# Window attention and a sticky mixture of experts on one core: a list's last products placed later in the order, the first branch target announced earlier, and the weight subtractions shared out evenly

## The chip, the core and the metric

The kernel runs on one core of a Trainium2 chip. The core has five engines with instruction streams of their own: TensorE (PE in the profile, its weight loads PEld), VectorE (DVE), ScalarE (ACT), GpSimd (POOL) and SyncE (SP). Streams wait for each other by semaphores. The metric is the device time of one execution in microseconds (us), the median of several.

## What is computed

An attention over 8 batches of 512 local and 32 global tokens gives 4608 rows `x` of 512 numbers. A sticky router then picks one of 8 experts for each row, and two products with that expert's weights make the output:

```python
fresh_e = int(np.argmax(logits[b, s]))
if s == 0 or local_gate[b, s] < 0.5:
    e = fresh_e
else:
    e = prev_e if prev_e >= 0 else fresh_e
prev_e = e
...
h = np.maximum(x[b, s] @ w1[e], 0.0)
out[b, s] = p[e] * (h @ w2[e])
```

`w1[e]` is 512 x 1024 and `w2[e]` 1024 x 512. Which rows go to which expert is known only when the attention and the router are done.

## The kernel before

**Two parts.** Class `Attn` works through the attention and `Route` sorts the rows by expert. `Moe` computes the experts in blocks of up to 256 rows (512 for what is left over): three early blocks (`NX = 3`) of rows that are known before the last batch is routed, then eight "rem" blocks, one for each expert's remainder, then as many full blocks as the data need. In this input there are three full ones.

**One block.** A weight matrix comes in eight pieces of 128 x 1024 floats (four of `w1`, four of `w2`). For each piece `load` issues a DMA on SyncE into a buffer `raw`; `split` lets ScalarE convert it to the rounded half `hi` (a CAST, L1143), and the next `flush` lets VectorE subtract (L1152) to get the rest `lo`. `flush` also issues the load of the next piece. The rows of a block are gathered by GpSimd (L1177), transposed on TensorE in groups of 128 (`xpose`, L1191) and split in the same way: ScalarE copies to `xh` (L1193), VectorE subtracts to `xl` (L1194). `mm1` then makes eight chunks of 12 matmuls (L1226), one for each 128 hidden columns; ScalarE applies the relu to `hh` (L1228), and VectorE makes the rest `hl` (L1229). The three PSUM banks that `mm1` rotates over come free by these two. `mm2` makes eight chunks of three matmuls (L1237) for each group of 128 rows. `store` scales the sum on ScalarE (L1242) and GpSimd scatters it (L1243).

**Order of the last early block.** The last batch's routing and the lists run as a generator, `tail`. After each chunk `hook` takes one step of it, flushes, and makes the splits that the table `SP` names. Inside `tail`, the generator `lists` is stepped twice per hook (`every(..., 2)`). It ends in `pick`: three VectorE operations make one-hots in a buffer in `xT` (L989, L991, L993), then after `wait` empty steps 34 small matmuls on TensorE sum them (L999), and two VectorE operations make the row numbers (L1001, L1002). A second, larger `pick` for the other lists ends at the very end of the third block. `kinds` makes `cnd`, the case of each rem block.

**Rem blocks.** Each rem block is a ten-way switch: `half` for up to 128 rows (case 0), otherwise `part` with `mm1` over 256 to 512 columns. What a case does is called its arm. After the arm, all cases join in the common part `close`: the last eight chunks of `mm2`, two transpositions for the next block, the gather for the block after it, and two splits. Before `close`, `hint` loads `cnd` of the next block into a register on all five engines and announces the branch target (TENSOR_LOAD L1403, BRANCH_PREFETCH_HINT L1409). The branch itself is a COMPARE_BRANCH, shown under L1532 together with other code that the framework adds. An arm makes six splits, `close` two. At the start of the first rem block the ring of `raw` buffers grows from four to eight.

## Time and profile before

| | |
|---|---|
| median of 3 runs | 723.16 us (722.44 to 723.32) |
| the profiled execution | 724.97 us, of which the span from the first to the last instruction is 723.2 us |
| granted TensorE clock, mean | 0.979 |
| TensorE busy | 675.5 us (93%) |
| VectorE, ScalarE, GpSimd busy | 436.8, 345.6, 192.8 us |

The attention fills the first 225 us. The early blocks follow to 333 us and the rem blocks from 336 us. A row of the timeline gives an instruction's start, its duration, its engine, line and operation, the tiles it writes and reads, and how many instructions are merged in the row; in brackets stand the idle time of its engine before it and what ended that. Names are by tile: weights and activations of the rem blocks share `wp`, `wq`, `xh`, `hh` and others by reuse of the memory.

### The profile page before, as it was taken

What the parts mean: (1) busy time and instruction counts of PE and PEld (TensorE: products, weight loads), DVE (VectorE), ACT (ScalarE), POOL (GpSimd) and SP (SyncE); (2) the same over time, 40 slices, a digit from 0 to 9 for tenths busy, and PEclk for the clock granted to TensorE, in tenths of its full rate; (3) what the DMA queues carried; (4) which work ended last, traced back from release to release, by engine and by line L of the source; (5) the groups of instructions that cost most, each with busy time, mean ns of one, the idle gap of its engine ahead of it and who ended that gap; (6) DMA issues with size and microseconds to landing.
All of it is one profiled execution on the core that took longest, in us unless ns stands there. A gap on an engine that the chain in (4) does not pass through costs nothing.

```text
span 723.2 us, 18483 instructions
## 1 busy us (share of the span) xinstructions
PE 675.5 (93%) x7253; PEld 563.5 (78%) x7253; DVE 436.8 (60%) x1142; ACT 345.6 (48%) x614; POOL 192.8 (27%) x321
## 2 busy tenths in 40 slices
PE   8999999999899899698997999999999999999990
PEld 6777777777567869586886888889788889899880
DVE  7868778778787777883527444426263525265660
ACT  4555555554445646352436444335344425255550
POOL 7634434334143110223022303040403020212210
PEclk9999999999999999899998999999999999999996
DMA  8866876966584576668238645445554433366762
GB/s 325 367 245 230 322 281 240 340 253 243 189 311 170 196 235 236 234 199 291 88 128 262 218 165 177 153 168 163 181 191 153 167 133 102 122 211 240 236 207 91
DMA packets 43444, 153.02 MB, mean 212 GB/s; under 512 B 8013, under 2 KB 9293, under 8 KB 39120
## 3 DMA queue, kind: packets, MB, share of 16 engines
q1 hardware_dynamic: 35968, 128.49, 50.2%
q0 software_dynamic: 6960, 21.90, 9.2%
q8 instruction: 77, 1.26, 0.7%
q14 instruction: 151, 1.24, 0.5%
q10 hardware_dynamic: 288, 0.13, 0.1%
HBM read 132.12 MB, written 19.69 MB: 210 GB/s over the span
## 4 chain that ended last, share of the span: by engine, by line
PE 32%; issue 22%; DVE 5%; POOL 3%; ACT 1%; SPq 1%; DMA 0%; POOLq 0%; ACTq 0%; DVEq 0%
PE ps L1237 16%; PE ps L1226 13%; POOL out_dram L1243 2%; PE ps L1191 1%; POOL xr L1177 1%; DVE wp L1152 1%; DVE wq L1152 1%; DMA raw<-in_w_dram 0%; SPq L417 0%; DVE wp L1194 0%; PE ps L999 0%; DVE hl L1229 0%; DVE hl L1152 0%; ACT wp L1143 0%; DVE o L905 0%
## 5 line engine op out<-in xcount | busy, mean ns | idle before, releaser
L1243 POOL DMA_INDIRECT out_dram<-y,tk x39 | 42.0, 1078 | 340.0 <-ACT y L1242 326.9
L1237 PE MATMUL ps<-wp,wq 128*128 128x512 f32 x504 | 128.4, 402 | 1.4 <-ACT wp L1143 1.4
L1226 PE MATMUL ps<-wp,wp 128*128 128x256 f32 (+5 forms) x672 | 111.1, 325 | 4.5 <-issue 2.9
L1226 PEld LDWEIGHTS ps<-wp,wp 128*128 128x128 f32 x672 | 104.8, 190 | 10.3 <-issue 3.5
L1237 PEld LDWEIGHTS ps<-wp,wq 128*128 128x128 f32 x504 | 93.5, 190 | 21.9 <-ACT wp L1143 1.8
L1229 DVE SCALAR_TENSOR_TENSOR wq<-ps,wq 128x256 fp32r<-128x256 f32 (+5 forms) x80 | 41.9, 527 | 98.9 <-ACT wq L1228 91.2
L1228 ACT ACTIVATE wq<-ps 128x256 fp32r<-128x256 f32 (+5 forms) x80 | 36.9, 467 | 89.3 <-PE ps L1226 85.8
L191 POOL TENSOR_SCALAR_AFFINE_SELECT qbd<-raw 64x512 f32<-64x512 f32 x62 | 44.6, 720 | 119.6 <-PE ps L243 101.8
L243 PE MATMUL ps<-kx,qbd 128*64 128x128 f32 x1024 | 71.1, 280 | 3.0 <-issue 2.6
L1242 ACT ACTIVATE y<-ps,pp 128x512 f32<-128x512 f32 x39 | 26.8, 688 | 85.7 <-PE ps L1237 83.9
L243 PEld LDWEIGHTS ps<-kx,qbd 128*64 128x64 f32 x1024 | 54.8, 137 | 12.7 <-issue 8.0
L248 DVE TENSOR_REDUCE mx<-ps 128x4 f32<-128x512 f32 x64 | 43.9, 686 | 29.6 <-PE ps L243 29.6
L1152 DVE TENSOR_TENSOR wp<-raw,wp 128x1024 fp32r<-128x1024 f32 x47 | 57.0, 1216 | 0.0
L254 ACT ACTIVATE pe<-pe 128x512 f32<-128x512 f32 x64 | 40.7, 636 | 32.7 <-DVE pe L250 32.7
L1143 ACT CAST wp<-raw 128x1024 fp32r<-128x1024 f32 x49 | 51.1, 1045 | 6.2 <-DMA raw<-in_w_dram 5.4
L1152 DVE TENSOR_TENSOR wp<-xT,wp 128x1024 fp32r<-128x1024 f32 x16 | 19.6, 1225 | 52.9 <-ACT wp L1143 52.9
L1177 POOL DMA_INDIRECT xr<-xs,idx x32 | 35.4, 1106 | 38.3 <-DVE L L391 17.5
L250 DVE TENSOR_TENSOR pe<-ps,mx 128x512 f32<-128x512 f32 x64 | 44.1, 688 | 1.6
L276 PE MATMUL ps<-v,pt 128*32 128x65 f32 x2048 | 42.6, 222 | 1.9 <-DVE xa L284 0.8
L276 PEld LDWEIGHTS ps<-v,pt 128*32 128x32 f32 x2048 | 33.3, 110 | 13.6 <-issue 7.4
L191 POOL TENSOR_SCALAR_AFFINE_SELECT kx<-raw 128x384 f32<-128x384 f32 (+3 forms) x127 | 42.9, 371 | 3.2 <-DMA raw<-in_qk_dram 1.1
L262 ACT COPY pt<-ps 128x512 f32<-128x512 f32 x64 | 34.9, 610 | 16.9 <-PE ps L260 16.9
(287 smaller groups left out, 1191.8 us busy)
## 6 DMA issues: line engine op xcount, KB each, us to landing
raw<-in_w_dram SPq DMA_DIRECT2D x79, 512.0 KB, 3.4
v<-in_vw_dram SPq DMA_DIRECT2D x32, 1040.0 KB, 8.0
raw<-in_qk_dram SPq DMA_DIRECT2D x32, 528.0 KB, 7.6
xa<-in_w_dram SPq DMA_DIRECT2D x24, 512.0 KB
xT<-in_w_dram SPq DMA_DIRECT2D x24, 512.0 KB
xs<-xa SPq DMA_DIRECT2D x8, 1056.0 KB, 4.5
qgb<-in_qg_dram SPq DMA_DIRECT2D x8, 128.0 KB, 4.8
out_dram<-y,tk POOLq DMA_INDIRECT x39, 4.4
```

The costliest lines, as they stand in the source:

```text
L191: self.nc.gpsimd.affine_select(out=out, in_=in_, pattern=pat, compare_op=ALU.is_ge, fill=0.0, base=0, channel_multiplier=0)
L243: nc.tensor.matmul(sp[64 * t2:64 * t2 + 64, t], qbd[:, w], kf[:, f:f + P], start=False, stop=True, skip_group_check=True)
L248: nc.vector.tensor_reduce(out=mx, in_=st["sp"], axis=AX.X, op=ALU.max)
L250: nc.vector.tensor_tensor(out=st["pe"][:, 4 * hb:4 * hb + 4], in0=st["sp"], in1=mx.broadcast_to([P, 4, P]), op=ALU.subtract)
L276: nc.tensor.matmul(o[32 * w4:32 * w4 + 32, g, h], pt[:, 2 * g + w4 // 2, w4 % 2, h, :], v[:, w, h * (D + 1):(h + 1) * (D + 1)], start=True ...
L1143: nc.scalar.copy(out=hi, in_=raw)
L1152: (nc.gpsimd if pool else nc.vector).tensor_tensor(out=lo, in0=raw, in1=hi.bitcast(F32), op=ALU.subtract)
L1177: self.nc.gpsimd.indirect_dma_start(out=self.xr[j], out_offset=None, in_=src, in_offset=bass.IndirectOffsetOnAxis(ap=self.rt.idx[:, c0 + j ...
L1226: nc.tensor.matmul(ph, a[:, dc, fs], b_[:, dc, n0:n1], start=(n == 0), stop=(n == 11))
L1229: nc.vector.scalar_tensor_tensor(out=hl[:, fc, n0:n1], in0=ph, scalar=0.0, in1=hh[:, fc, n0:n1].bitcast(F32), op0=ALU.max, op1=ALU.subtract)
L1237: nc.tensor.matmul(py, a[:, fc, js], b_[:, fs], start=(fc == 0 and k == 0), stop=(fc == 7 and k == 2))
L1243: sc = nc.gpsimd.indirect_dma_start(out=self.out, out_offset=bass.IndirectOffsetOnAxis(ap=self.g[1][:, j:j + 1], axis=0), in_=y, in_offset ...
```

## The change

1. The first `pick` gets `wait = 12` instead of 2. With two steps of the list per hook, its matmuls come five chunks later on TensorE, and everything of the tail behind it moves as well.
2. In the third early block, `kinds` is run to its end and `hint(i + 1)` is issued after the first chunk of the second row group and not inside its sixth. This puts the hint ahead of the four transpositions for the first rem block.
3. The splits of a rem or full block are now four in the arm and four in `close`, in place of six and two. In `close` the splits come after the transpositions. The last split of `close` is subtracted in the next block's arm.
4. In rem and full blocks the loads no longer follow the subtractions (`eager = False`). The arm issues eight loads, one per chunk of `mm1` except the fifth, and the last in the first chunk of `mm2`. The four extra loads at the end of the third early block go.
5. All four groups of a rem block are gathered into one tile `xr4`, and the three small VectorE operations for each group of rows (the product with the expert's one-hot, the token number, the sum) are done once for all groups (`scals`), at the end of `close`, and not after each transposition.

```diff
-        yield from self.pick(cid, phi, self.o2, 0, 4, 2 * NX, ((0, NT),), po)
+        yield from self.pick(cid, phi, self.o2, 0, 4, 2 * NX, ((0, NT),), po, 12)
...
+        self.eager = True
...
     def flush(self):
         nc = self.nc
-        for pool, raw, hi, lo in self.pend:
+        while self.pend:
+            pool, raw, hi, lo = self.pend.pop(0)
             (nc.gpsimd if pool else nc.vector).tensor_tensor(out=lo, in0=raw, in1=hi.bitcast(F32), op=ALU.subtract)
-            self.load()
-        self.pend = []
-
-    def step(self, n=0):
+            if self.eager:
+                self.load()
+
+    def step(self, n=0, loads=0):
         self.flush()
         for _ in range(n):
             self.split()
+        for _ in range(loads):
+            self.load()
...
+        if i < NX:
+            self.scal(i, j, xr.rearrange("p (o r) -> p o r", o=1))
+
+    def scal(self, i, j, xr):
...
+    def scals(self, i):
+        if i < NSLOT:
+            self.scal(i, 0, self.xr4[:, 0:4 if self.kind(i) == "rem" else 2])
...
         for fc in range(8):
-            if mid and fc == 4:
+            if mid and fc == 1:
                 while not self.known:
                     self.take(next(self.tail))
-            if mid and fc == 6:
                 self.hint(i + 1)
             self.mm2(i, py, fc, 1, *x[2:])
             self.hook(i, 16 + fc)
             if mid and fc in XPM:
                 self.xpose(i + 1, XPM.index(fc))
+                if fc == XPM[-1]:
+                    self.scals(i + 1)
...
+            self.eager = False
             old = [self.raw() for _ in range(4)]
             self.raw.t, self.raw.k = self.more + old, 0
-            for _ in self.more:
-                self.load()
...
-            self.step((2, 1, 1, 1)[k])
+            self.step(1, 2 if k < 3 else 1)
         for j in range(2):
             self.xpose(i + 1, j)
         turn(3)
-        self.step(1)
-        self.step()
+        self.step(0, 1)
...
             self.mm1(i, fc, *x, n0, n1)
-            self.step(fc % 2 == 0)
+            self.step(fc % 2 == 0, fc != 4)
...
                 if g == 0:
-                    self.step(fc in (1, 4))
+                    if fc == 0:
+                        self.step(0, 1)
                     if fc in (2, 5):
                         self.xpose(i + 1, fc // 3)
...
             self.mm2(i, py, fc, j, self.HH, self.HL)
-            self.step(fc in (1, 4))
             if fc in (2, 5):
                 self.xpose(i + 1, 2 + fc // 3)
                 if fc == 5:
+                    self.scals(i + 1)
                     self.gather(i + 2)
+            self.step(fc in (1, 3, 5, 7))
         self.store(py, j)
```

TensorE, the end of the second early block. `ps_64` is the sum of its second row group, two rows a chunk; `L999` are the first list's matmuls, of which the first pair stands here. Before:

```order
L1237 MATMUL ps_64<-wp_100,hh 128x512 x2
L1237 MATMUL ps_64<-wp_100,hl 128x512
L1237 MATMUL ps_64<-wp_101,hh 128x512 x2
L1237 MATMUL ps_64<-wp_101,hl 128x512
L999 LDWEIGHTS o_290
L999 MATMUL ps_69<-xT,o_290 128x8
```

TensorE at the same place now:

```order
L1253 MATMUL ps_64<-wp_101,hh 128x512 x2
L1253 MATMUL ps_64<-wp_101,hl 128x512
L1253 MATMUL ps_64<-wp_4207,hh 128x512 x2
L1253 MATMUL ps_64<-wp_4207,hl 128x512
L1253 MATMUL ps_64<-wp_4207,hh 128x512 x2
L1253 MATMUL ps_64<-wp_4207,hl 128x512
L1253 MATMUL ps_64<-wp_4208,hh 128x512 x2
L1253 MATMUL ps_64<-wp_4208,hl 128x512
L1253 MATMUL ps_64<-wp_4208,hh 128x512 x2
L1253 MATMUL ps_64<-wp_4208,hl 128x512
L999 LDWEIGHTS o_290
L999 MATMUL ps_69<-xT,o_290 128x8
```

The list's matmuls stood after the third chunk of the group and now stand after its eighth, the last one of the block.

VectorE, from the last `hl` of the third early block to the first `xl` of the first rem block (`wp_4311` from `ps_68`). Before:

```order
L1229 SCALAR_TENSOR_TENSOR hl<-ps_65,hh 128x256
L1152 TENSOR_TENSOR wp_4207<-raw_79,wp_4207 128x1024
L1229 SCALAR_TENSOR_TENSOR hl<-ps_66,hh 128x256
L1152 TENSOR_TENSOR wp_4208<-raw_80,wp_4208 128x1024
L1152 TENSOR_TENSOR wp_4312<-raw_77,wp_4312 128x1024
L1152 TENSOR_TENSOR wp_4313<-raw_78,wp_4313 128x1024
L1152 TENSOR_TENSOR xl<-raw_79,xh 128x1024
L1194 TENSOR_TENSOR wp_4311<-ps_68,wp_4209 128x4x128
```

VectorE now, from a little behind the last `hl` (the second large one-hot group and one of the weight subtractions stand ahead of this piece):

```order
L993 TENSOR_SCALAR xT<-xT,ipf 128x8x54
L989 TENSOR_TENSOR xT<-cid,phi 128x8x54
L991 TENSOR_TENSOR xT<-xT,t_264 128x8x54
L993 TENSOR_SCALAR xT<-xT,ipf 128x8x54
L1155 TENSOR_TENSOR wp_4312<-raw_77,wp_4312 128x1024
L1155 TENSOR_TENSOR wp_4313<-raw_78,wp_4313 128x1024
L1155 TENSOR_TENSOR xl<-raw_79,xh 128x1024
L1420 TENSOR_LOAD cnd
L1426 SWITCH_STRIDE
L1426 ISA
L1426 BRANCH_PREFETCH_HINT
L1199 TENSOR_TENSOR wp_4311<-ps_68,wp_4209 128x4x128
```

Of the second list's one-hots, which all stood ahead of the last two `hl`, these and some more are now behind them, and the hint has come between the subtractions and the first `xl`.

ScalarE, `close` of the first rem block; `y` are the two stores of the block, L1193 (now L1198) the copies of the transposed rows. Before:

```order
L1242 ACTIVATE y_4318<-ps_70,pp_92 128x512
L1143 CAST wp_4312<-xT 128x1024
L1193 CAST wp_4209<-ps_68 128x4x128
L1143 CAST wp_4313<-xT 128x1024
L1193 CAST wp_4209<-ps_67 128x4x128
L1242 ACTIVATE y_4316<-ps_63,pp_92 128x512
L1532 SWITCH_STRIDE
```

ScalarE in the same `close` now:

```order
L1258 ACTIVATE y_4318<-ps_70,pp_92 128x512
L1145 CAST wp_4207<-xa_109 128x1024
L1198 CAST wp_4209<-ps_68 128x4x128
L1145 CAST wp_4208<-xa_109 128x1024
L1198 CAST wp_4209<-ps_67 128x4x128
L1145 CAST wp_4312<-xT 128x1024
L1145 CAST wp_4313<-xT 128x1024
L1258 ACTIVATE y_4316<-ps_63,pp_92 128x512
L1549 SWITCH_STRIDE
```

Two conversions that the arm made have come here, and the last two conversions now stand between the second copy and the second store.

## Prediction

> **What bounds the kernel now.** I read the page first, then TensorE's timeline with the idle time ahead of each row, then the clock in stretches.

> ```profile
> span 723.2 us, 18483 instructions
> PE 675.5 (93%) x7253; PEld 563.5 (78%) x7253; DVE 436.8 (60%) x1142; ACT 345.6 (48%) x614; POOL 192.8 (27%) x321
> ```

> TensorE is busy 93% of the span, so a change that removes no matmuls can only win back its idle time and its slow clock. From the end of the second early block on, these are the long waits of TensorE:

> ```profile
> 298.81 1.05 PE L999 MATMUL ps<-xT,o 128*128 128x8 bf16 x34 [6.70 <-DVE xT L993]
> ...
> 314.11 1.21 PE L1226 MATMUL ps<-xh,wp 128*128 128x256 f32 x8 [0.63 <-DVE hl L1229]
> ...
> 317.83 0.73 PE L1237 MATMUL ps<-wq,hh 128*128 128x512 f32 x2 [0.55 <-DVE hl L1229]
> ...
> 336.05 9.21 PE L1226 MATMUL ps<-wp,wp 128*128 128x480 f32 x34 [2.90 <-issue]
> ```

> ```profile
> 390.19 0.66 PE L1191 MATMUL ps<-idf,xr 128*128 128x128 f32 x4 [1.10 <-DVE wq L1338]
> 391.65 0.96 PE L1191 MATMUL ps<-idf,xr 128*128 128x128 f32 x4 [0.81 <-DVE wq L1338]
> 393.38 0.69 PE L1335 MATMUL ps<-idf,gsb 128*128 128x128 f32 x2 [0.77 <-DVE wp L1194]
> 395.48 3.82 PE L1237 MATMUL ps<-wp,wq 128*128 128x512 f32 x9 [1.41 <-ACT wp L1143]
> ...
> 410.80 2.19 PE L1226 MATMUL ps<-wp,hl 128*128 128x352 f32 x12 [0.90 <-DVE wq L1229]
> ...
> 523.31 1.86 PE L1226 MATMUL ps<-wp,wp 128*128 128x288 f32 x12 [1.49 <-DVE wq L1229]
> ```

> Together 17.3 us: 6.70 at the first list, 2.90 at the first switch, 4.09 in the one `half` arm, and the rest where a product waits for `hl`. Three of these waits also cost clock:

> ```profile
> 296.29:299.70 3.41, 0.89 (x34) 0.89 (x34) 3.26 (x6) 1.05 (x1) 2.42 (x1) 0.50 0.66 232
> 299.70:303.12 3.42, 3.42 (x14) 2.74 (x12) 3.15 (x9) 0.00 (x0) 0.00 (x0) 0.50 0.80 260
> ...
> 337.25:340.66 3.41, 3.41 (x10) 2.84 (x9) 0.00 (x0) 0.43 (x1) 1.66 (x2) 0.50 0.95 323
> ...
> 391.86:398.69 6.83, 4.65 (x14) 3.17 (x13) 5.29 (x12) 1.90 (x3) 0.00 (x0) 0.50 0.87 287
> ```

> The first number behind the comma is TensorE's busy time, the 0.50 near the end its granted clock. Work at half clock loses half its time: (0.89 + 3.42) / 2 = 2.15 us after the first list, 3.41 / 2 = 1.7 after the first switch, 4.65 / 2 = 2.3 in the `half` arm.

> **Part 1, the later list.** TensorE waits for the one-hots, which VectorE finishes in the first row below. Nothing ahead of them on VectorE is moved, so they will be ready at the same time.

> ```profile
> 298.22 0.53 DVE L993 TENSOR_SCALAR xT<-xT,ipf 128x136 bf16<-128x136 bf16 x1
> ...
> 303.44 0.63 PE L1237 MATMUL ps<-wp,hh 128*128 128x512 f32 x2
> 303.91 0.39 PE L1237 MATMUL ps<-wp,hl 128*128 128x512 f32 x1
> 304.14 0.63 PE L1237 MATMUL ps<-wp,hh 128*128 128x512 f32 x2
> ```

> A chunk takes 304.14 - 303.44 = 0.70 us. Five now run inside the wait: 3.5 us gained, 3.2 us of the wait left. The clock should still fall, since the 2.90 us at the first switch were enough for that; one stretch of 3.41 us at half clock costs 1.7 where 2.15 were lost (0.45 gained). [...] The two short waits for `hl` (0.63 and 0.55) I count as gone, because another takes their place: VectorE now has to finish its work sooner.

> ```profile
> 298.40:326.89 28.49, 26.90 (x186) 23.76 (x186) 21.97 (x44) 12.02 (x19) 6.31 (x7) 0.92 0.69 221
> ...
> 331.82 0.69 DVE L1194 TENSOR_TENSOR wp<-ps,wp 128x512 fp32r<-128x512 f32 x1 [0.99 <-ACT wp L1193]
> ```

> From the one-hots to the first `xl` of the rem blocks, VectorE has 21.97 us of work (the fourth column), and the hint now stands ahead of that `xl`; the hint's price is the 0.99 us idle before the second row, where it stood. 298.40 + 21.97 + 0.99 = 321.4, and 0.69 for the `xl`: 322.1 at the earliest. TensorE now starts the third block at 298.81 + 1.05 = 299.9. Its `mm1` takes 8 x 1.40 = 11.2 (chunks start at 310.52 and 311.92, rows below), the next group 8 x 0.70 = 5.6, and the third transposition, which needs the bank that the first `xl` frees, comes after six more chunks and two transpositions of 0.44: 299.9 + 11.2 + 5.6 + 4.2 + 0.9 = 321.8, or 323.5 with the 1.7 of slow clock.

> ```profile
> 310.52 1.10 PE L1226 MATMUL ps<-xh,wp 128*128 128x256 f32 x8
> ...
> 311.92 1.10 PE L1226 MATMUL ps<-xh,wp 128*128 128x256 f32 x8
> ```

> ```profile
> 325.80 0.44 PE ps L1191 x4
> ```

> If VectorE never idles there is no wait in the slow case. But it must wait for products in `mm1`, and the last one-hots stand behind the last `hl`; following both orders step by step I get 2.2 us. I take 1.5, nearer to the second. Part 1: -3.5 - 0.45 - 1.2 + 1.5 = **-3.65 us**. Ends: -6.9 with no new wait and full clock (3.5 + 2.15 + 1.2); -0.9 if the short waits stay, the new one is 2.2 and costs another half stretch of slow clock (-3.95 + 2.2 + 0.85).

> **Part 2, the earlier hint.** TensorE's sequencer runs ahead of its products. These are its branches into an arm, and the hints before them (one instruction each; durations in ns, then the start):

> ```profile
> L1409 PEldq BRANCH_PREFETCH_HINT  x1: 39/39/39, 329.3 to 329.3; - x1
> ...
> L1532 PEldq COMPARE_BRANCH  x1: 3465/3465/3465, 332.4 to 332.4; - x1
> ...
> L1409 PEldq BRANCH_PREFETCH_HINT  x1: 36/36/36, 507.1 to 507.1; - x1
> ...
> L1532 PEldq COMPARE_BRANCH  x1: 3423/3423/3423, 513.1 to 513.1; - x1
> ...
> L1532 PEldq COMPARE_BRANCH  x1: 1481/1481/1481, 546.5 to 546.5; - x1
> ```

> The first branch takes 3.47 us, 3.1 after its hint, and the queue is nearly empty because the second list's 34 matmuls ahead of it are short: hence the 2.90 idle. In `close`, with a hint six us ahead, one branch takes 3.42 and one 1.48. The first hint now stands seven chunks, four transpositions and the list ahead of the branch: at least 8 us. I take 1.5 us for the branch, as in the better case: 2.0 less idle, and with under 1 us idle the clock stays up: 1.7. Part 2: **-3.65 us**. Ends: 0 (the hint does nothing) and -4.6 (2.90 + 1.7). [...] SyncE's four loads move behind its own branch; their data are first split in `close`, a whole arm later, so they cost nothing.

> **Part 3, four splits in `close`.** The chain through the slowest of these transitions:

> ```profile
> 516.80 0.04 ACT y L1242
> ...
> 517.04 5.11 issue
> ...
> 522.28 0.42 ACT wq L1228
> ...
> 522.80 0.47 DVE wq L1229
> ```

> ```profile
> 513.49 1.05 ACT L1143 CAST wp<-xT 128x1024 fp32r<-128x1024 f32 x1
> 515.33 0.59 ACT L1193 CAST wp<-ps 128x512 fp32r<-128x512 f32 x1 [0.78 <-PE ps L1191]
> ```

> ScalarE can branch only when its last store is on its way (517.00), then fetches code for 5.11 us, and the first relu and `hl` follow; TensorE has by then used its three banks and waits 1.49. Now two conversions come between the copy at 515.33 and the store: 515.33 + 0.59 + 2 x 1.05 = 518.0 less some overlap, against 516.80: 0.9 later. So each arm whose three first chunks end before `hl` comes loses up to 0.9.

> ```profile
> 482.47 4.02 PE L1226 MATMUL ps<-wp,wp 128*128 128x352 f32 x24
> ...
> 487.67 0.53 DVE L1229 SCALAR_TENSOR_TENSOR wq<-ps,wq 128x352 fp32r<-128x352 f32 x1 [4.81 <-ACT wq L1228]
> ```

> At 523.31 (288 columns) it is the full 0.9. Here, 482.47 + 1.5 x 4.02 = 488.5 against 488.2: 0.3 of slack, 0.6 lost. For the two arms of 448 columns, whose chunks are 27% longer, I put 0.3 each. The 2.4 us wait at 523.31 may now cost a stretch of clock, 0.6 x 1.7 = 1.0. Part 3: **+3.1 us**; ends 0 (the branches get cheaper as arms get shorter) and +6.

> **The `half` arm** has four conversions instead of six, so its closing product starts about 2.6 us (two of 1.05 and a subtraction's share) ahead of 395.48. But ScalarE then has four in `close` before its branch:

> ```profile
> 395.43 2.45 issue
> ...
> 404.65 5.42 issue
> ```

> The fetch in the first row follows the arm's last conversion, so it ends 2.1 us earlier, at 395.43 + 2.45 - 2.1 = 395.8. Four conversions, two copies and two stores (4 x 1.05 + 2 x 0.59 and an estimated 0.7 for each store) end at 402.6, 2.05 ahead of 404.65, and the product that resumed at 410.80 resumes by as much earlier. I take 1.75, since the stores also wait for TensorE; less 1.0 for a stretch of slow clock behind a wait that grows by 2.6 - 1.75: **-0.75 us**, ends -1.75 and +1.0. The merged small VectorE operations are off the path: 0.

> **Sum.** -3.65 - 3.65 + 3.1 - 0.75 = -4.95, say -4.7 with both clock shares rounded. The profiled execution took 724.97 (span 723.2 and 1.8 around it), so it would take 720.3. It lies 1.8 above the median of the runs, 723.16; the forecast for the median is **718.5 us**.

> **The rivals.**
> - *The hint does nothing* (part 2 is 0): 722.1. For it: 3.42 after six us. Against it: 1.48 at the same distance.
> - *ScalarE's conversions decide* (slower). In the `close` before each of the three narrow arms (410.80, 482.47, 523.31) both conversions stand in the way in full, 2.1 us, and the wait drops the clock, 1.7: 11.4 us in all. With parts 1 and 2 as forecast (-7.3) and the `half` arm at -0.75 that is +3.35: 726.5. It decides once a narrow arm loses over 2.7 us. Against it: the 0.78 us idle ahead of the copy at 515.33, which a conversion can fill.
> - *The clock stays full* behind the 3.2 us wait and the waits of part 3: 718.5 - 1.7 - 1.0 = 715.8. [...]

> **How the numbers follow.** Chances: forecast 0.50, hint without effect 0.26, ScalarE decides 0.13, clock stays full 0.11. The forecast's own range is 715.5 to 721.5 (part 1 alone has 3 us to either side). The range to hold 8 in 10 runs from 714.5 to 724.0: it takes in the first and third rivals and leaves out the slower one. A measurement here tells apart about 0.2% (721.7 to 724.6 is the same): faster takes most of the forecast, half of the first rival and the third, 0.71; same 0.15; slower 0.14.

> **What would show it.** Right: the list's matmuls wait about 3.2 us; the third transposition of the first rem block's rows waits for `xl`; TensorE's first arm branch takes about 1.5 us and its clock is full behind it; the row at 523.31 shows a wait of about 2.4. Wrong: an arm branch still at 3.4 us, several half-clock stretches behind 400 us, or narrow arms that wait over 3 us.

## The result, and the profile after

The changed kernel takes **717.4 us** (median of 4 runs, 715.54 to 717.84); the kernel before took 722.91 beside it (722.44 to 723.32). The ratio is **0.9919, with a 95% interval of 0.9900 to 0.9938**: 5.9 us faster. Forecast was 718.5. The total was right; of the terms of its sum, one held and the others did not, and their errors cancel. The rest of this document is mostly about that.

The profiled execution of after took 717.19 us, 7.8 less than that of before (724.97). Not all of that is the change. The same transposition inside the unchanged attention and early blocks, first in before, then in after:

```profile
256.56 0.66 PE L1191 MATMUL ps<-idf,xr 128*128 128x128 f32 x4
```

```profile
252.67 0.66 PE L1196 MATMUL ps<-idf,xr 128*128 128x128 f32 x4
```

After is 3.89 us ahead here, where nothing has been edited. The start of the first list's products, which the last batch's routing sets, lay between 294.2 and 300.2 us in fourteen profiled executions. VectorE, for which these products wait, has the same work up to there in all of them, so this is scatter between executions. To compare traces I therefore count from that start (298.81 in before, 295.10 in after) to the end of the span: 424.4 us before, 420.3 after. Runs of one kernel differ by more than these 4.1 us (the kernel before took 716.9 to 726.7 us in 22 runs on one chip); so what is said of an edit's worth rests on the ratios, and the traces are for the places.

TensorE's waits in after, for the same places as in the prediction:

```profile
295.10 1.00 PE L999 MATMUL ps<-xT,o 128*128 128x8 bf16 x34 [3.27 <-DVE xT L993]
...
320.74 0.66 PE L1196 MATMUL ps<-idf,xa 128*128 128x128 f32 x4 [0.83 <-DVE wp L1199]
...
327.30 20.91 PE L1242 MATMUL ps<-wp,wp 128*128 128x480 f32 x96 [2.45 <-issue]
...
379.44 0.63 PE L1196 MATMUL ps<-idf,xa 128*128 128x128 f32 x4 [0.90 <-DMA xa<-xs,idx]
...
382.34 1.08 PE L1196 MATMUL ps<-idf,xa 128*128 128x128 f32 x4 [2.28 <-DMA xa<-xs,idx]
...
384.37 4.10 PE L1253 MATMUL ps<-wp,wq 128*128 128x512 f32 x9 [0.52 <-ACT wq L1353]
...
402.47 3.89 PE L1242 MATMUL ps<-wp,hl 128*128 128x352 f32 x12 [3.64 <-DVE wq L1245]
...
511.33 4.98 PE L1242 MATMUL ps<-wp,wp 128*128 128x288 f32 x36 [0.87 <-ACT wp L1145]
...
516.52 1.85 PE L1242 MATMUL ps<-wp,wp 128*128 128x288 f32 x12 [0.21 <-DVE wq L1245]
```

The list's wait is halved, as forecast (3.2), and a short wait for `xl` has appeared, as forecast. But at the first switch 2.45 us of idle time are left of 2.90, where 0.9 were forecast. In the `half` arm two waits are new, for rows that a gather is still bringing. And the arm of 288 columns, which was to wait 2.4 us, waits 0.87 and 0.21. The stretches at 0.5 of the clock, and the one behind the first switch:

```profile
296.04:299.45 3.41, 3.41 (x19) 3.41 (x17) 2.52 (x5) 0.38 (x1) 2.59 (x2) 0.50 0.83 256
327.30:330.70 3.40, 3.40 (x16) 3.00 (x17) 0.00 (x0) 0.53 (x2) 2.66 (x3) 1.00 0.96 337
381.37:388.20 6.83, 5.34 (x15) 4.18 (x16) 2.20 (x4) 0.86 (x2) 0.18 (x1) 0.50 0.96 329
401.85:408.68 6.83, 6.21 (x21) 6.21 (x22) 5.31 (x7) 0.46 (x1) 0.95 (x1) 0.50 0.78 248
```

One stretch of 3.41 us stays behind the list, as forecast. The clock behind the first switch is full in this execution, although the idle time hardly shrank. In and behind the `half` arm stand two slow stretches of 6.83 us where before had one.

### The profile page after: what moved, and what is told of

It reads as the page before. It is cut to its first block, busy times and chain, and to the rows that moved or that the text cites. A ratio compares the mean times of both kernels' runs of the same rounds, so it can differ in the third digit from the quotient of the medians.

```text
span 715.4 us, 18380 instructions
## 1 busy us (share of the span) xinstructions
PE 674.5 (94%) x7253; PEld 565.9 (79%) x7253; DVE 426.9 (60%) x1057; ACT 343.7 (48%) x614; POOL 199.3 (28%) x321
## 5 line engine op out<-in xcount | busy, mean ns | idle before, releaser
L1259 POOL DMA_INDIRECT out_dram<-y,tk x39 | 48.0, 1232 | 287.7 <-ACT y L1258 259.7
L1242 PE MATMUL ps<-wp,wp 128*128 128x256 f32 (+5 forms) x672 | 110.8, 325 | 3.5 <-issue 2.5
L1242 PEld LDWEIGHTS ps<-wp,wp 128*128 128x128 f32 x672 | 105.0, 191 | 8.9 <-issue 3.9
L1199 DVE TENSOR_TENSOR wp<-ps,wp 128x512 fp32r<-128x512 f32 x40 | 27.5, 690 | 106.9 <-ACT wp L1198 106.8
L1182 POOL DMA_INDIRECT xa<-xs,idx x42 | 46.6, 1110 | 59.9 <-issue 41.8
L1198 ACT CAST wp<-ps 128x512 fp32r<-128x512 f32 x40 | 23.5, 588 | 58.1 <-PE ps L1196 58.0
```

What stands on the lines that cost most here:

```text
L1182: self.nc.gpsimd.indirect_dma_start(out=self.xr[j] if k == "early" else self.xr4[:, j], out_offset=None, in_=src, in_offset=bass.IndirectO ...
L1242: nc.tensor.matmul(ph, a[:, dc, fs], b_[:, dc, n0:n1], start=(n == 0), stop=(n == 11))
L1259: sc = nc.gpsimd.indirect_dma_start(out=self.out, out_offset=bass.IndirectOffsetOnAxis(ap=self.g[1][:, j:j + 1], axis=0), in_=y, in_offset ...
```

## The experiments

All times are ratios to the kernel before on the same chip, with 95% intervals; a ratio is turned into us with 722.9. "To the end" is the profiled span less the start of the first list's products, as above (before: 424.4).

| kernel | parts | ratio | us | to the end |
|---|---|---|---|---|
| after | 1 to 5 | 0.9919 [0.9900, 0.9938] | -5.9 | 420.3 |
| after_b | 1 to 5 again | 0.9929 [0.9897, 0.9961] | -5.1 | 419.9 |
| e1_pick | 1 | 0.9952 [0.9929, 0.9976] | -3.5 | 422.5 |
| e2_hint | 2 | 1.0016 [0.9984, 1.0048] | +1.2 | 426.2 |
| e3_rest | 3, 4, 5 | 0.9949 [0.9919, 0.9978] | -3.7 | 419.0 |
| e4_fourbuf | 1, 2, 3, 4 | 0.9984 [0.9956, 1.0013] | -1.2 | 421.3 |
| e5_lateloads | 1, 2, 3, 5 | 0.9947 [0.9920, 0.9974] | -3.8 | 422.8 |
| e6_earlyloads | 4 | 0.9927 [0.9902, 0.9952] | -5.3 | 419.7 |
| e7_nohint | 1, 3, 4, 5 | 0.9914 [0.9882, 0.9946] | -6.2 | 415.9 |
| e9_fourloads | four loads of part 4 | 0.9959 [0.9935, 0.9982] | -3.0 | 421.7 |
| e8_pickloads | 1, 4 | 0.9891 [0.9857, 0.9924] | -7.9 | 415.3 |
| e10_pick16 | 1 (wait 16), 4 | 0.9884 [0.9849, 0.9920] | -8.4 | 416.1 |
| e11_split | 1, 3, 4 | 0.9995 [0.9968, 1.0023] | -0.4 | 419.9 |

### The parts apart

**The list alone.** The edit, on the kernel before:

```diff
-        yield from self.pick(cid, phi, self.o2, 0, 4, 2 * NX, ((0, NT),), po)
+        yield from self.pick(cid, phi, self.o2, 0, 4, 2 * NX, ((0, NT),), po, 12)
```

> The kernel before with part 1 alone (the first list's products five chunks later). Theory A (the parts add up as the two traces suggest): the wait ahead of the list's products falls from 6.7 to about 3.2 us, one stretch of 3.41 us stays at half clock, the third transposition waits 0.8 us for xl, and the first switch keeps its 2.9 us and its slow stretch: 3.0 to 3.9 us faster, 719.0 to 719.9. Theory B (most of the 5.5 us between the medians is an early start of this stage that has nothing to do with the edits, since the attention ended 3.8 us sooner in the trace of after): 0 to 2 us faster.

Measured: 0.9952, so 3.5 us faster, theory A (the interval, 1.7 to 5.1 us, still touches theory B's 0 to 2; the waits decide for A). TensorE's rows in this kernel:

```profile
297.51 1.05 PE L999 MATMUL ps<-xT,o 128*128 128x8 bf16 x34 [3.28 <-DVE xT L993]
...
324.19 0.66 PE L1191 MATMUL ps<-idf,xa 128*128 128x128 f32 x4 [1.02 <-DVE wp L1194]
```

The wait fell to 3.28, and the third transposition pays 1.02. The first switch cost 3.34 us of idle time here, with its slow clock. One sign of theory A is missed: behind the list two stretches stay at half clock (6.83 us from 297.19 us on), not one.

**The hint alone.**

```diff
-            if mid and fc == 4:
+            if mid and fc == 1:
                 while not self.known:
                     self.take(next(self.tail))
-            if mid and fc == 6:
                 self.hint(i + 1)
```

> The kernel before with part 2 alone (cases known and announced after the first chunk of the last row group). Theory A: TensorE's first arm branch still takes over 3 us, so its idle time stays between 2.4 and 2.9; only the clock behind it may stay up: 0 to 1.8 us faster. Theory B (the prediction's): the branch takes 1.5 us, 3.7 us faster, 719.2. Theory C: the kinds' operations, run early, delay VectorE's one-hots behind them: slower by up to 1 us.

Measured: 1.0016, no gain; a gain of over 1.2 us is outside the interval. TensorE's branch, and the wait behind it:

```profile
L1531 PEldq COMPARE_BRANCH  x1: 3422/3422/3422, 331.3 to 331.3; - x1
```

```profile
334.88 1.46 PE L1226 MATMUL ps<-wp,wp 128*128 128x480 f32 x4 [2.86 <-issue]
```

The branch takes 3.42 us where it took 3.47, and 2.86 us stay idle. Theory B, the prediction's, has fallen. A 16 KB packet of code, of the DMA queue q8 (kind `instruction`), starts 0.9 us behind the start of this branch.

**Everything else.** The changed kernel with the old list (`wait` 2) and the old place of the hint, so parts 3, 4 and 5 alone. Against the changed kernel:

```diff
-        yield from self.pick(cid, phi, self.o2, 0, 4, 2 * NX, ((0, NT),), po, 12)
+        yield from self.pick(cid, phi, self.o2, 0, 4, 2 * NX, ((0, NT),), po)
...
-            if mid and fc == 1:
+            if mid and fc == 4:
                 while not self.known:
                     self.take(next(self.tail))
+            if mid and fc == 6:
                 self.hint(i + 1)
```

> The kernel with parts 3, 4 and 5 alone (four splits in the arm and four in close, early loads, one gather tile), the list and the hint as before. Theory A: the half arm and the arm behind it lose what the two traces show between their branches (about 4.9 us), the other arms win 1.2 and the last arm nothing: 3 to 4 us slower, 726 to 727. Theory B (the loss in the half arm comes from its meeting with the earlier start of the arm, and the later arms' gain is worth more): within 1.5 us of before.

Measured: 0.9949, 3.7 us *faster*. Theory A added up the two traces of single executions and has the wrong sign. Theory B's range (1.5 us) is missed too. In the trace the first switch waits only 1.28 us, its branch takes 1.84, and no slow stretch follows. The merged VectorE operations of part 5 stand ahead of the first switch too, but what TensorE waits for there is its own branch, and beside that the four loads ahead of it are gone. That gave the next theory (C), a guess at this point: a taken branch fetches code through the same DMA engines as the loads, and part 4 takes the loads out of its way.

**Four gather buffers again.** The changed kernel without part 5: four separate buffers, and the small operations after each transposition.

```diff
-    moe.xr4 = at.xa.t[0]
+    moe.xr += [at.xa.t[0][:, k] for k in range(2)]
...
-        xr = self.xr[j] if i < NX else self.xr4[:, j]
+        xr = self.xr[j]
```

> The changed kernel with part 5 undone: four separate buffers for the gathered row groups, and the three small VectorE operations after each transposition. Theory A (the gathers of the block behind the half arm wait for the last transposition and the merged small operations, and land too late): the two waits for gathered rows (0.90 and 2.28 us) go, the old short waits come back in part: 1 to 3 us faster than the changed kernel, 714.4 to 716.4. Theory B (the gathers are late because the eight early loads share the DMA engines with them): the waits stay within 0.5 us of 3.2, and so does the time, 717.4.

On the waits theory A is right, on the time it is wrong. GpSimd's first gather of the rows in question, in before and then in after:

```profile
378.63 0.99 POOL L1177 DMA_INDIRECT xr<-xs,idx  x1 [0.30 <-issue]
```

```profile
373.46 1.35 POOL L1182 DMA_INDIRECT xa<-xs,idx  x1 [5.67 <-PE ps L1362]
```

In before the gather of the first group starts 4.0 us ahead of the `half` arm's first product (382.58). In after it starts 1.4 us behind it (372.04), because one tile serves all four groups and the last transposition and the merged operations have to be done with it. In this kernel the two waits for rows are gone from the `half` arm. Yet it stands at 0.9984, against 0.9919 and 0.9929 of the changed kernel; the arms of 352 and 288 columns wait 1.58 and 2.21 us, as the prediction's part 3 had it. The last experiment takes this up.

### The loads

**The changed kernel again**, as a base.

> The changed kernel once more, as the base of this call. Its ratio to the kernel before should again be 0.990 to 0.994. If the time of code fetches is set by what the DMA engines carry then, VectorE's branches from an arm into close take 2.7 to 3.0 us again (kernel before: 3.6 to 4.5); if they are accidents of one execution, they scatter over 2.5 to 4.5. The wait of the products behind the half arm (3.64 us and a slow stretch) tells in the same way whether it belongs to the kernel or to that execution.

The ratio repeats (0.9929). So do the branches: VectorE's seven from an arm into `close` (leaving out the `half` arm) take 2.70 to 2.96 us. The wait behind the `half` arm is 2.15 us and its slow stretch 3.41, so of the 3.64 us and 6.83 in the first trace a part belongs to that execution, not to the kernel.

**Early loads alone**, on the kernel before: eight loads in the arm, none behind the subtractions, none ahead of the first switch. Splits stay at six and two, the buffers at four.

```diff
-            self.step(fc % 2 == 0)
+            self.step(fc % 2 == 0, fc != 4)
...
-            for _ in self.more:
-                self.load()
+            self.eager = False
```

> The kernel before with part 4 alone: eight loads early in the arm, none in close, none ahead of the first switch; splits six and two, four gather buffers. Theory C: VectorE's branches into close fall to 2.7 to 3.0 us, the first switch's idle time falls below 2 us and its slow stretch goes: 2 to 4 us faster than before. Theory D: within 1 us of before. The prediction (SyncE's loads cost nothing either way): within 0.5 us of before.

Measured: 0.9927, 5.3 us faster, above the upper end that theory C gave. By itself this part is worth as much as the whole change. VectorE's branches from arms into `close`, each a stretch from the branch to its next instruction; the last two columns are the share of the DMA engines' time and GB/s. Before, after, and early loads alone:

```profile
427.29:431.81 4.52, 4.52 (x21) 3.68 (x20) 0.09 (x1) 0.59 (x1) 1.01 (x1) 1.00 0.57 193
465.18:469.40 4.22, 4.22 (x20) 3.41 (x19) 0.10 (x1) 0.58 (x1) 1.01 (x1) 1.00 0.57 207
504.74:509.25 4.51, 4.51 (x21) 3.66 (x20) 0.09 (x1) 0.63 (x1) 1.00 (x1) 1.00 0.63 213
517.04:522.04 5.00, 4.78 (x36) 4.55 (x35) 0.00 (x0) 0.46 (x1) 2.92 (x3) 1.00 0.95 303
```

```profile
420.91:423.63 2.72, 2.72 (x13) 2.23 (x13) 0.62 (x1) 0.69 (x1) 1.00 (x1) 1.00 0.04 14
458.51:461.31 2.80, 2.80 (x13) 2.26 (x13) 0.63 (x1) 0.69 (x1) 1.00 (x1) 1.00 0.03 10
497.82:500.54 2.72, 2.72 (x13) 2.19 (x13) 0.62 (x1) 0.69 (x1) 1.00 (x1) 1.00 0.05 14
511.28:515.68 4.40, 4.35 (x33) 4.38 (x34) 0.94 (x1) 1.08 (x3) 3.24 (x3) 1.00 0.91 285
```

```profile
421.96:424.82 2.86, 2.86 (x14) 2.32 (x13) 0.09 (x1) 0.60 (x1) 1.00 (x1) 1.00 0.23 72
...
500.15:502.92 2.77, 2.77 (x14) 2.23 (x13) 0.09 (x1) 0.63 (x1) 1.00 (x1) 1.00 0.17 58
```

With quiet DMA engines (a share of 0.03 to 0.23) the fetch takes 2.72 to 2.86 us, with 0.57 to 0.63 it takes 4.2 to 4.5. Three later arms of before took 3.7 and 3.9 us at 0.6 and 3.60 at 0.81, so the share alone does not give the length. The fourth row of before and of after is a branch the other way, into an arm: there loads and gathers are under way in both kernels, and the fetch takes 5.00 and 4.40. The gain in the time is not in the branches into `close`, behind which TensorE has work enough, but where TensorE has nothing to do while it lasts: at the first switch, and at the very end. The end in before and with early loads, by the last store's scatter:

```profile
705.97 1.02 POOL L1243 DMA_INDIRECT out_dram<-y,tk  x1 [1.95 <-ACT y L1242]
```

```profile
700.93 1.02 POOL L1247 DMA_INDIRECT out_dram<-y,tk  x1 [1.97 <-ACT y L1246]
```

From it to the end of the span are 723.2 - 706.0 = 17.2 us in before and 715.5 - 700.9 = 14.6 here. In before 426 packets of weight loads, for a block that no longer comes, are still moved after 700 us; here none. All fourteen traces fall apart in this way: 16.2 to 17.3 us where such loads are under way (before, and the kernels e1, e2, e5 and e9), 14.1 to 14.9 in the other nine.

**Late loads again**, the changed kernel without part 4:

```diff
-            self.eager = False
...
+            for _ in self.more:
+                self.load()
...
-        for _ in range(loads):
-            self.load()
```

> The changed kernel with part 4 undone: each load follows a subtraction again, so four of eight are issued in close, and four more are issued ahead of the first switch. Theory C (a taken branch fetches code over the same DMA engines as the loads, and part 4 clears them before the branches): VectorE's branches into close rise from 2.8 to 3.6 to 4.5 us, SyncE's and ScalarE's too, and the first switch costs TensorE 2.9 us or more: 2 to 4 us slower than the changed kernel. Theory D (the fetch has nothing to do with the loads; the even split is what wins): within 1 us of the changed kernel.

Theory C's numbers are met only in part. The first switch costs 2.47 us with a branch of 3.04 and a slow stretch, as it said. But VectorE's branches into `close` stay at 2.70 to 3.00: with the even split the loads that follow subtractions no longer fall on them. And 0.9947 against 0.9929 is 1.3 us in a comparison that tells apart some 3. So with the even split the early loads are worth less than on the kernel before, and how much is open.

**The hint late**, the changed kernel with the hint in its old place:

```diff
-            if mid and fc == 1:
+            if mid and fc == 4:
                 while not self.known:
                     self.take(next(self.tail))
+            if mid and fc == 6:
                 self.hint(i + 1)
```

> The changed kernel with part 2 undone: the first case is read and announced late, as before. The run of part 2 alone gave nothing, so within 1 us of the changed kernel, with TensorE's first arm branch between 1.8 and 3.5 us as in all kernels so far. The prediction's step (the early hint shortens the branch by 2 us and keeps the clock): 3 to 4 us slower than the changed kernel.

0.9914: the same as the changed kernel within the interval, and not the 3 to 4 us slower that the prediction's step needs. TensorE's branch takes 1.81 us, the wait 1.25, and the clock stays full. Over all kernels without the four loads, the first branch took 0.77, 0.98, 1.84, 1.81, 2.00 and 1.90 us with the late hint (0.44 in the kernel with wait 16), and 3.02, 2.52 and 2.54 with the early one; with the four loads 3.46 and 3.90 late, 3.42 and 3.04 early. The early hint is, if anything, the worse one: it costs TensorE's branch about 1 us.

The kept traces show where that goes. In 97 of the 98 branches of TensorE into an arm other than `half`, in all fourteen traces, the branch ends 1.34 to 1.54 us after a 16 KB packet of q8 has landed. So in these traces the branch's end goes with the packet's landing, and the question is when the packet starts. At the first switch, behind the late hint and without the four loads, it starts 1.3 to 2.8 us after the hint and 0.4 to 3.0 us ahead of the branch; with the four loads, 4.0 and 4.6 us after the hint, which is behind the start of the branch. Behind the early hint it starts only with the branch or up to 0.9 us later, 11.3 to 12.0 us after the hint, with the loads and without. So code was fetched ahead behind the late hint and not behind the early one. What makes the early one fail was not tried.

### What carries the gain

**Only the four loads** ahead of the first switch are moved, on the kernel before:

```diff
-            for _ in self.more:
-                self.load()
...
             self.step(fc % 2 == 0)
+            if i == NX and fc < 4:
+                self.load()
```

(and one in each step of `half`, should the first block take that case.)

> The kernel before with one thing changed: the four extra loads that the third early block issues ahead of the first switch are issued in the first rem block's arm. All other loads, the list, the hint, the splits and the gather buffers are as before. Theory C (code is fetched over the DMA engines, and these four loads hold up the fetch at the first switch): TensorE's first arm branch falls from 3.4 to 3.9 us to under 2 us, the idle time there from 2.9 to under 1.3, and the slow stretch behind it goes: 2.5 to 4 us faster. Theory D (what parts 4 and 3 win comes from the later arms): TensorE's first branch stays above 3 us, within 1 us of before.

Measured: 0.9959, 3.0 us faster; theory C. DMA traffic around the branch in before (332.4 to 336.0 us) and here (329.5 to 331.0), then TensorE's branch and first product here:

```profile
q1 hardware_dynamic: 268, 0.97, 90.7%
q8 instruction: 1, 0.02, 1.9%
q14 instruction: 1, 0.01, 0.5%
```

```profile
q14 instruction: 1, 0.01, 2.0%
```

```profile
L1534 PEldq COMPARE_BRANCH  x1: 980/980/980, 329.5 to 329.5; - x1
```

```profile
330.66 0.69 PE L1226 MATMUL ps<-wp,wp 128*128 128x480 f32 x2 [0.41 <-issue]
```

The columns of the first two are packets, MB and the share of 16 engines. In before the packets of code stand among 268 of the weight loads, whose packets took 90.7% of the 16 engines' time; here nothing but code moves. The 16 KB packet had landed at 329.03 us here, ahead of the branch; in before it started at 333.37, 0.9 us behind the branch. The branch takes 0.98 us for 3.47, the idle time is 0.41 for 2.90, and the slow stretch is gone. This is the gain that the prediction gave to the hint. With the 2.6 us at the end of the program, which this kernel does not win (17.0 us there), these 3.0 make 5.6, against the 5.3 that the early loads are worth.

**The list and the early loads**, parts 1 and 4 alone: the kernel with early loads, and

```diff
-        yield from self.pick(cid, phi, self.o2, 0, 4, 2 * NX, ((0, NT),), po)
+        yield from self.pick(cid, phi, self.o2, 0, 4, 2 * NX, ((0, NT),), po, 12)
```

> The kernel before with parts 1 and 4 (later list, early loads), without the earlier hint, the even split and the one gather tile. If parts 1 and 4 carry the whole gain and add up: 0.985 to 0.990 of before, faster than the changed kernel by 2 to 4 us. If the even split and the one tile are needed as well: 0.991 to 0.994, as the changed kernel.

0.9891, 7.9 us faster than before; the two parts alone were worth 3.5 and 5.3, together 8.8. It is the better kernel by its median: the changed one stood at 0.9919 and 0.9929. The intervals overlap, so that it is faster than the changed kernel is likely and not shown.

**The list two chunks later still**, with early loads:

```diff
-        yield from self.pick(cid, phi, self.o2, 0, 4, 2 * NX, ((0, NT),), po, 12)
+        yield from self.pick(cid, phi, self.o2, 0, 4, 2 * NX, ((0, NT),), po, 16)
```

> As the kernel with parts 1 and 4, with the list's products two chunks later still (wait 16 for 12), so that two chunks of 1.4 us fill most of the 3.3 us that were left. Theory A (VectorE's 22 us from the one-hots to the first xl set the pace behind it): the wait at the list falls below 1 us and its slow stretch goes, but the third transposition then waits 3 to 5 us for xl: within 1 us of the kernel with parts 1 and 4. Theory B (TensorE sets the pace): 3 to 4.5 us faster than that kernel.

0.9884, within 1 us of the last one. TensorE's rows:

```profile
294.21 1.00 PE L999 MATMUL ps<-xT,o 128*128 128x8 bf16 x34 [0.29 <-DVE xT L993]
...
297.69 1.21 PE L1230 MATMUL ps<-xh,wp 128*128 128x256 f32 x8 [0.96 <-DVE hl L1233]
...
317.64 0.66 PE L1195 MATMUL ps<-idf,xa 128*128 128x128 f32 x4 [1.93 <-DVE wp L1198]
```

The list's wait is down to 0.29 us and its slow stretch is gone, but 0.96 for `hl` and 1.93 for `xl` have come, with a slow stretch behind the latter (319.7 to 323.1 us). From the list's start to the start of the first arm's branch it took 29.2 us for 29.5, so what the list gave up has gone to these waits. To the branch's end it took 29.6 for 31.5, because the branch took 0.44 us for 2.00; its code packet had landed 2 us ahead of the branch. At the end nothing of it is left (416.1 for 415.3): the arms of 352 and 288 columns wait 4.58 us for 2.62. Theory A names what takes over, VectorE, and was too high on the wait for `xl` (3 to 5 us).

### The even split by itself

The last run, parts 1, 3 and 4: the even split without the one tile, to be held against parts 1 and 4. It is the changed kernel with four gather buffers, as above, and the hint late:

```diff
-            if mid and fc == 1:
+            if mid and fc == 4:
...
+            if mid and fc == 6:
                 self.hint(i + 1)
```

> The kernel with parts 1, 3 and 4 (later list, even split, early loads), with four gather buffers and the hint late. Beside the kernel with parts 1 and 4 alone (0.989 of before) it tells what the even split costs without the one tile. Theory A (the prediction's step on the conversions: they make ScalarE's last store late, and the narrow arms pay): 3 to 6 us slower than parts 1 and 4, 0.993 to 0.998 of before, with waits over 1.2 us in the arms of 352 and 288 columns. Theory B (the even split costs nothing; the kernel with four buffers and the early hint was slow through the hint): 0.987 to 0.991, with those waits under 1 us.

Measured: 0.9995 against 0.9891, a difference of 0.0104 with some 0.0043 of uncertainty: 4.4 to 10.7 us slower. TensorE's waits, of this kernel and then of the one without the even split:

```profile
402.39 3.54 PE L1241 MATMUL ps<-wp,hl 128*128 128x352 f32 x12 [3.22 <-DVE wq L1244]
...
482.88 0.91 PE L1241 MATMUL ps<-wp,xh 128*128 128x352 f32 x4 [1.58 <-DVE wq L1244]
...
512.06 4.97 PE L1241 MATMUL ps<-wp,wp 128*128 128x288 f32 x36 [0.89 <-ACT wp L1145]
...
519.17 1.85 PE L1241 MATMUL ps<-wp,wp 128*128 128x288 f32 x12 [2.14 <-DVE wq L1244]
```

```profile
400.87 2.19 PE L1230 MATMUL ps<-wp,hl 128*128 128x352 f32 x12 [1.58 <-DVE wq L1233]
...
507.81 5.02 PE L1230 MATMUL ps<-wp,wp 128*128 128x288 f32 x36 [0.45 <-issue]
...
513.42 1.86 PE L1230 MATMUL ps<-wp,wp 128*128 128x288 f32 x12 [0.59 <-DVE wq L1233]
```

The narrow arms wait 7.83 us in the one and 2.62 in the other. The time and the places are theory A's. This profiled execution took 718.6 us, 4.5 below the median of its kernel, so its trace shows the place and not the whole of the loss.

The mechanism of theory A, the prediction's, is not what the traces show. ScalarE and then VectorE at the last of these arms, whose first product starts at 512.06; then their first results without the even split, where it starts at 507.81:

```profile
L1549 ACTq COMPARE_BRANCH  x1: 43/43/43, 511.5 to 511.5; - x1
512.19 0.69 ACT L1257 ACTIVATE y<-ps,pp 128x512 f32<-128x512 f32 x1
516.15 0.41 ACT L1243 ACTIVATE wq<-ps 128x288 fp32r<-128x288 f32 x1 [3.27 <-PE ps L1241]
512.23 6.26 issue
518.66 0.46 DVE L1244 SCALAR_TENSOR_TENSOR wq<-ps,wq 128x288 fp32r<-128x288 f32 x1 [5.49 <-ACT wq L1243]
```

```profile
512.39 0.41 ACT L1232 ACTIVATE wq<-ps 128x288 fp32r<-128x288 f32 x1 [4.26 <-issue]
512.91 0.46 DVE L1233 SCALAR_TENSOR_TENSOR wq<-ps,wq 128x288 fp32r<-128x288 f32 x1 [5.36 <-ACT wq L1232]
```

ScalarE branches at 511.5, while its last store (512.19) still stands behind the conversions: the branch did not wait for the store here. The first relu comes 4.1 us after the arm's first product, for 4.6 without the even split. It is VectorE that is late. Its fetch, the row of 6.26 us, took 4.74 in the other kernel, and its first `hl` comes at 6.6 us for 5.1. In the arms of 448, 352 and 448 columns ScalarE's last store is later by the forecast 0.9 us (1.2 us after the first product, for 0.25 in before), yet its branch starts at 0.5 in both. VectorE's branch starts 1.2 us after the first product, for 0.5 to 0.7 without the even split, and takes 4.9 to 5.6 us for 4.1 to 4.6.

With the one tile beside the even split (parts 1, 3, 4 and 5, the kernel without the hint) the ratio is 0.9914 again: the tile gives back 5.9 us, with an uncertainty of 3.1. The same pair with the early hint (four gather buffers against the changed kernel) gives 4.0 to 4.7. Its waits at 288 columns are 0.23 and 0.51. What the tile saves is again on VectorE: in the arms of 448, 352 and 448 columns its branch starts 0.96 us after the first product for 1.2, and its branches into the last five rem arms take 4.4 to 6.3 us with four buffers and 3.7 to 4.8 with one tile, whose gathers are issued later. That the gathers are out of the way of these fetches is a guess that no run tests by itself.

## Why the prediction was right, and where it was not

| step | forecast, us | measured, us | how |
|---|---|---|---|
| 1, later list | -3.65 | -3.5 | list alone |
| 2, earlier hint | -3.65 | +1.2 (-1.2 to +3.5) | hint alone |
| loads moved | 0 | -5.3 | early loads alone |
| 3, four splits in `close` | +3.1 | +7.5 (4.4 to 10.7) | parts 1, 3, 4 against 1, 4 |
| merged operations, one tile | 0 | -5.9 (-2.8 to -8.9) | parts 1, 3, 4, 5 against 1, 3, 4 |
| the `half` arm | -0.75 | in the rows above | |
| sum | -4.95 | -5.9 | the changed kernel |

The measured parts add up to -3.5 + 1.2 - 5.3 + 7.5 - 5.9 = -6.0. In part this is so by construction: the rows for the splits and for the tile lead from the kernel with parts 1 and 4 to the one without the hint. What the sum tests is that parts 1 and 4 add up (8.8 us apart, 7.9 together) and that the hint gives nothing.

**Part 1 held, but for the clock.** A wait of 3.2 us at the list (3.27), the short waits for `hl` gone, and a new wait for `xl` of 1.5 (0.83; 0.64 to 1.02 in the other traces with this part and the same `wait`). The one slow stretch came in two of the eight traces with `wait` 12; in the other six, the second trace of the changed kernel among them, it is two stretches, as in before, so the 0.45 us that the sum counted for it mostly did not come. The rival "the clock stays full" is not borne out at this place: a slow stretch followed this wait in every kernel with `wait` 12.

**Part 2 failed at its first step**: "I take 1.5 us for the branch, as in the better case". The branch's length was read as a matter of the hint's distance, from a 3.42 and a 1.48 at the same distance, which by themselves said that something else decides. What differs is when the packet of code starts: 1.1 us behind the start of the branch of 3.42, 0.9 ahead of the branch of 1.48. At the first switch the four loads held it up (it started 4.0 us after the hint in before, and had landed ahead of the branch once they were moved), and their traffic stood in the profile. The rival "the hint does nothing" had part 2's worth, but left the loads out, and the hint in its old place is followed by an early fetch once they are gone. The full clock that part 2 promised did come, from 327.30 us on, by chance: the section on the hardware shows how near it was.

**The loads** got one sentence: "SyncE's four loads move behind its own branch; their data are first split in `close`, a whole arm later, so they cost nothing." It asked when the data are needed, and not what the transfers hold up. This is the largest miss, and it lies on the good side.

**Part 3** had the places (the arms of 352 and 288 columns, a wait of 2.4 us at 288: 2.14 and 2.21 in the two kernels that have part 3 without part 5), but not the mechanism, and its size was less than half of what was measured. The step that failed is "ScalarE can branch only when its last store is on its way": the store came 0.9 us later, as forecast, and neither the branch nor the first relu did. VectorE came later instead, by its own branch and its fetch. In the changed kernel most of this doesn't show because of part 5, which "off the path: 0" left out. The rival in which ScalarE's conversions decide (+3.35 in all) was near in time without the one tile, but not in its cause.

**The `half` arm** should have closed 2.6 us sooner. From its first product to the closing one it took 395.48 - 382.58 = 12.9 us, and 384.37 - 372.04 = 12.3 now. The other 2.0 went into the waits for gathered rows, 0.90 and 2.28 us (1.56 and 1.03 in the second trace), which come from the one tile; the prediction looked at the operations that are merged and not at the transfers that must wait for them. The arm behind it did not resume 2.05 us sooner either. That step took the row 404.65 for ScalarE's fetch, and it is VectorE's (the row ahead of it in the same view is VectorE's branch, DVEq L1532). ScalarE's first relu did come sooner, 23.9 us after the `half` arm's first product for 26.3; but the product waits for VectorE, and resumed after 30.4 us for 28.2 (28.7 in the second trace).

**The signs** that the prediction named split in the same way. The list's wait and the wait for `xl` came, the full clock in one trace of two; a first branch of 1.5 us (3.02) and a wait of 2.4 at 288 columns (0.21) did not. Two signs against it came: an arm branch of 4.15 us, and a narrow arm that waits 3.64 (2.15 in the second trace).

So the total was right by luck, through cancelling: the hint's -3.65 did not come, and -5.3 from the loads, not counted, did; the split cost 4.4 more than its +3.1, and the tile, not counted, gave 5.9 back.

## What to carry to other kernels

A load that is moved has two prices: when its data are needed, and what else moves while it runs; here that was the code for a branch (3.47 us with the four loads ahead of it, 0.98 without). When two rows of one mechanism differ by a factor of two at the same setting, look for the second cause before taking the better one. When one buffer replaces four, ask what refills it and which reader comes last. And before pricing a delay on one engine, check which engine's result the waiting product needs last.

## What the runs showed of the hardware

**Code comes in DMA packets, and the fetches were longer beside loads.** VectorE's fetch behind a branch into `close` took 2.7 to 3.0 us at a DMA share up to 0.3 (after, and early loads alone) and 3.6 to 4.5 at 0.57 to 0.81 (before). In the row 465.18:469.40 of before two packets of code (q14) stand among 220 of the loads' queue (q1), in 420.91:423.63 of after three among 4. TensorE's branch at the first switch took 0.98 for 3.47 (rows above), and ended 1.34 to 1.54 us after a 16 KB packet of code had landed, there and in nearly all later arms. By which path the loads hold the code up, no run shows.

```profile
323.34:326.76 3.42, 1.51 (x32) 1.35 (x29) 1.28 (x6) 0.66 (x1) 1.62 (x2) 1.00 0.52 193
326.76:330.17 3.41, 2.87 (x13) 2.55 (x14) 0.00 (x0) 0.00 (x1) 2.50 (x4) 1.00 0.94 314
```

```profile
327.09:330.50 3.41, 1.46 (x9) 1.20 (x7) 0.42 (x2) 0.00 (x0) 2.24 (x3) 1.00 0.47 131
330.50:333.91 3.41, 3.41 (x11) 2.78 (x10) 0.00 (x0) 0.67 (x2) 2.16 (x3) 0.50 1.06 370
```

A wait of 2.45 us that the grid cuts in two (1.91 idle and 0.54) was followed by full clock; a shorter one of 1.95 that lies in one stretch, by half clock. In the fourteen traces, from 286 us on and without the end of the program, each of the 37 stretches at full clock with up to 1.50 us of busy time was followed by half clock, and none of those with over 1.8 us; of six between 1.51 and 1.67 us, four were. So by these counts what follows a wait of about 2 us is a matter of luck here; waits of 1.25 to 1.43 us at this switch cost no clock in four kernels.
